# A one-core kernel for a long convolution gated with product-key experts: first loads reordered, first fold ahead of its scale, and another count of matmul time in the recording loop

## The chip, the core and the metric

The kernel runs on one core of a Trainium2 chip, as one program. The metric is the time of one execution on the device in microseconds (us). Five engines work beside each other, each through its own queue of instructions in a fixed order, and meet at semaphores: TensorE (PE; PEld is its loading of weights), VectorE (DVE), ScalarE (ACT), GpSimd (POOL) and SyncE (SP), which here only issues DMA transfers. Matmuls write to PSUM, of which this kernel uses eight banks of 128 x 512 f32.

## What is computed

The input x is one sequence of 2048 tokens with 576 channels. Two results are mixed by a gate.

```python
x = A_u
g = _sigmoid((x * gate_w).sum(-1, keepdims=True))
a = _A_ref(...)   # long convolution along the tokens, by FFT, + u * Dskip
b = _B_ref(...)   # experts
return g * a + (1 - g) * b
```

Part a makes a filter K of 2048 taps for each channel from 128 complex states, `K = einsum("dn,dnl,dn->dl", Cc, exp(logdA * l), dB).real`, and convolves it with the tokens. Part b asks 4096 experts through two tables of 64 keys, for 32 heads:

```python
q = jnp.einsum("nd,dhc->nhc", xf, w_q)
s1 = jnp.einsum("nhd,ed->nhe", q[..., :dk], k1)
s2 = jnp.einsum("nhd,ed->nhe", q[..., dk:], k2)
# the two best of s1 and of s2, the two best of their four sums: expert numbers top_e, weights g
act = _gelu(jnp.einsum("nd,nhkd->nhk", xf, u[top_e]))
out = jnp.einsum("nhk,nhk,nhkd->nd", g, act, v[top_e])
```

## The kernel before

**What is multiplied.** Nearly every product in f32 is made of f16 parts: an operand is scaled by a power of two and split into a high part and a low part (high = scaled value rounded to f16, low = what is left), and three matmuls per 128 of the 576 channels give the product. The last 64 channels go into two more. So a group of scores or of expert products is 14 matmuls of 128 x 512 (`triple`).

**Names.** The reader needs these, since the profile goes by them. `xs`, `xr` are a block of 512 tokens as loaded (first 512 channels, last 64 twice), `xb` the scaled and split block; there are four blocks (tb 0 to 3). `wq` is half a set of 8 columns of query weights (4 x 576 f32), `kt` the keys. Query weights and keys are folded into one matrix before they meet the tokens: matmuls `wb` of `wq` with `kt` (64 x 64 each), then a scale, then the parts `whl` (high, low) and `wrem` (last 64 channels). The scale of a fold needs the sum of squares of the weights (ACT writes `wj` and a sum, TensorE adds it over the partitions in `wn`). `us`, `ur` are 512 expert rows as loaded, `uhl` their parts, `sq` the sum of squares for their scale. `s` is a group of scores (c, t: fold c of 8, token tile t of 16); its reader on VectorE is MAX8 into `m` and FIND_INDEX8 into `i`. `a` is a group of products of tokens and expert rows (c, tb, j); its reader scales it to `go`, which is stored to `g_d` in HBM. `kP`, `CS`, `e`, `Y`, `kb`, `ko` are the steps that generate the filter, 18 pairs of channel chunks, spread over VectorE, ScalarE and GpSimd; `u` and `uh` the first step of the transform of the tokens. Later come `k` (transform of the filter), `pr`, `pi`, `pv` (product of the transforms), `tr` (transposing the chosen indices), `A`, `Be`, `Bg` (one-hot matrices from the indices, built on VectorE), `S` (their product: the weight of each expert), `gl` (gelu of the products, times S), `wh` (its parts), `vhl` (the parts of the expert values), `o` (output, `wh` times `vhl`) and `y` (the last transform of part a, with tables `tf` and rows `yz` loaded from HBM; `ya` is its sum).

**What sets the order.** The kernel is a Python program that records instructions, and the order in which it records them is the order in each engine's queue. A loop over `groups` (128 groups of scores) and `acts` (128 groups of expert products) records TensorE's main stream. It keeps a clock of its own: `mm` adds to `clock[0]` an estimated time for each matmul and a charge where the shape of the stationary operand changes, `Engine` estimates when VectorE, ScalarE and GpSimd are through, `dma` when a transfer lands. All else (building blocks, folds, the filter, the transforms) are generators in a heap; each yields until its operands are ready by these estimates (`ready`) or a bank or slot is free (`need`), and is then resumed by `pump` between matmuls. So the estimates never change what is computed, but they set where each instruction stands. Slots in SBUF (nine of 8 KB per partition) and banks have quotas by tag (`sc`, `kb`, `wb`, `slot`, `raw`).

**The start.** It loads keys, the first half of fold 0's query weights, the constants, token block 0, the second half of the weights and the first expert rows, in that order. `x_build` takes its block as an argument; `x_rest` loads and builds blocks 1 to 3 one after the other once block 0 is done. In `w_half` the matmuls of the fold come after the scale is known and with all banks from one tag.

## Time and profile before

| | |
|---|---|
| median of the runs | 1479.43 us (1478.44 to 1482.02) |
| the profiled execution | 1478.13 us, of which its span 1476.3 us |
| busy, share of the span: TensorE, VectorE, ScalarE, GpSimd | 97%, 85%, 53%, 36% |
| mean granted clock of TensorE | 0.995 |
| idle time of TensorE, sum | 42.0 us |
| HBM read, written | 147.51 MB, 71.30 MB |

Rows of the profile read as follows. A row of the order of time has start, length, engine, line, operation, output <- inputs, shape and count; in square brackets stands how long the engine had been idle and what ended that. Nearly all lines are 213 (matmul), 133 (the other engines) and 204 (DMA), since helpers record everything, so one goes by the tile names. A row of waits has the total in us, how many times, and the longest. A row of a table by stretches has the stretch, its length, the busy time of PE, PEld, DVE, ACT and POOL, each with its number of instructions, then the granted clock of TensorE (1.00 is full), the busy share of the DMA engines and GB/s.

### The profile page before, as it was taken

To read this page: it belongs to the slowest core of one execution; us is meant where nothing else is said; L and a number is where in the kernel's file an instruction comes from. 1 tells how busy PE (TensorE), PEld (TensorE's weight loads), DVE (VectorE), ACT (ScalarE), POOL (GpSimd) and SP (SyncE) were. 2 spreads that over 40 slices of the span, in tenths; PEclk is the share of its full clock that TensorE was granted. 3 is DMA by queue.
4 is the path that set the end of the run, shared out by engine and by line. 5 is a ranking of instruction groups with operands and counts; after the bars stand their busy time and mean duration, and the time that the engine had idled before them with its cause. 6 is when DMAs were issued, how large, how long until landed. Compare 5 with 4: busy or idle time off the path is not lost.

```text
span 1476.3 us, 36780 instructions
## 1 busy us (share of the span) xinstructions
PE 1434.3 (97%) x14024; PEld 861.1 (58%) x14028; DVE 1254.2 (85%) x4589; ACT 786.0 (53%) x1310; POOL 537.7 (36%) x513
## 2 busy tenths in 40 slices
PE   5999999999999999999999999999999999999999
PEld 3444544454455544555554444456787788788787
DVE  6989899989988899598997997589998998898860
ACT  6558778677686866625655644664424324323310
POOL 0454663634726465202247999522010110110100
PEclk9999999999999999999999999999999999999999
DMA  6443542443344343466576758676532442442400
GB/s 227 133 121 103 173 129 76 151 134 94 107 130 147 108 133 122 132 218 234 177 269 228 267 192 258 208 245 186 191 119 92 131 144 70 151 146 67 154 9 17
DMA packets 139184, 221.20 MB, mean 150 GB/s; under 512 B 11648, under 2 KB 82688, under 8 KB 132608
## 3 DMA queue, kind: packets, MB, share of 16 engines
q1 hardware_dynamic: 138912, 218.78, 46.2%
q8 instruction: 110, 1.80, 0.5%
q14 instruction: 66, 0.54, 0.1%
q10 hardware_dynamic: 96, 0.07, 0.0%
HBM read 147.51 MB, written 71.30 MB: 148 GB/s over the span
## 4 chain that ended last, share of the span: by engine, by line
PE 73%; DVE 19%; DMA 3%; ACT 2%; issue 2%; SPq 0%; POOL 0%; DVEq 0%; ACTq 0%
PE o L213 23%; PE a L213 19%; PE s L213 17%; DVE i L133 4%; PE S L213 4%; DVE m L133 3%; PE wb L213 2%; DVE e L133 2%; PE kb L213 2%; DVE uhl L133 2%; PE pr L213 1%; DVE Y L133 1%; DVE CS L133 1%; PE y L213 1%; DVE uh L133 1%
## 5 line engine op out<-in xcount | busy, mean ns | idle before, releaser
L213 PE MATMUL o<-vhl,wh 128*128 128x288 f16 x3072 | 387.3, 286 | 0.0
L213 PE MATMUL s<-whl,xb 128*128 128x512 f16 x1536 | 366.4, 381 | 5.9 <-DVE whl L133 3.5
L213 PE MATMUL a<-xb,uhl 128*128 128x512 f16 x1536 | 362.4, 380 | 4.1 <-DVE i L133 4.1
L213 PEld LDWEIGHTS <-wh 128*128 128x128 f16 x3072 | 295.9, 98 | 76.4 <-issue 3.7
L213 PEld LDWEIGHTS <-xb 128*128 128x128 f16 x1792 | 171.4, 98 | 211.4 <-issue 20.8
L213 PEld LDWEIGHTS <-uhl 128*128 128x128 f16 x1536 | 147.9, 98 | 178.7 <-issue 5.7
L133 DVE FIND_INDEX8 i<-m,s 128x8 uint32<-128x64 f32 x1024 | 206.5, 223 | 0.0
L133 ACT ACTIVATE wh<-gl,s_wg 128x1024 f16<-128x1024 f32 x63 | 67.6, 1137 | 206.8 <-DVE gl L133 206.8
L133 DVE MAX8 m<-s 128x8 f32<-128x64 f32 x1024 | 146.3, 215 | 24.6 <-PE s L213 23.3
L133 POOL TENSOR_TENSOR CS<-CS,ex 128x512 f32<-128x512 f32 x72 | 100.6, 1427 | 153.5 <-DVE ex L133 144.3
L133 POOL TENSOR_TENSOR ya<-ya,db 128x576 f32<-128x576 f32 x16 | 31.8, 1994 | 341.2 <-DVE Bg L133 151.2
L133 DVE SCALAR_TENSOR_TENSOR wh<-gl,s_wg,wh 128x1024 f16<-128x1024 f32 x64 | 90.6, 1447 | 11.3 <-ACT wh L133 11.3
L133 DVE TENSOR_TENSOR gl<-S,gl 128x256 f32<-128x256 f32 x256 | 90.0, 415 | 10.2 <-PE S L213 9.2
L133 POOL TENSOR_TENSOR e<-aN,rt 128x512 f32<-128x512 f32 x72 | 86.4, 1221 | 31.8 <-PE kb L213 31.7
L133 ACT ACTIVATE go<-a,i_a 128x512 f32<-128x512 f32 x95 | 64.4, 683 | 52.1 <-PE a L213 35.2
L133 DVE TENSOR_TENSOR Bg<-Be,vals 128x1024 f16<-128x1024 f16 x128 | 89.6, 741 | 2.2
L133 ACT ACTIVATE gl<-gl 128x1024 f32<-128x1024 f32 x64 | 63.5, 1045 | 44.8 <-DMA gl<-g_d 41.4
L133 DVE TENSOR_TENSOR A<-iota_a,vals 128x2048 f16<-128x2048 f16 x64 | 79.9, 1249 | 0.0
L213 PE MATMUL s<-wrem,xb 128*128 128x512 f16 x256 | 76.7, 381 | 0.1
L213 PE MATMUL a<-xb,wrem 128*128 128x512 f16 x256 | 76.2, 379 | 0.0
L213 PE MATMUL S<-Bg,A 128*128 128x64 f16 x2048 | 73.1, 193 | 2.6 <-DVE Bg L133 2.4
L213 PEld LDWEIGHTS <-A 128*128 128x128 f16 x2048 | 70.8, 97 | 7.7 <-issue 1.8
(202 smaller groups left out, 2225.2 us busy)
## 6 DMA issues: line engine op xcount, KB each, us to landing
g_d<-go SPq DMA_DIRECT2D x128, 256.0 KB, 2.5
gl<-g_d SPq DMA_DIRECT2D x32, 1024.0 KB, 5.7
wq<-in_wq_dram SPq DMA_DIRECT2D x16, 1152.0 KB, 7.1
us<-in_au_dram SPq DMA_DIRECT2D x64, 144.0 KB, 3.0
su_d<-us SPq DMA_DIRECT2D x32, 288.0 KB, 2.7
sk_d<-k1o SPq DMA_DIRECT2D x32, 288.0 KB, 3.0
vn<-in_vv_dram SPq DMA_DIRECT2D x32, 288.0 KB, 3.2
ui<-su_d SPq DMA_DIRECT2D x16, 576.0 KB, 4.2
```

The costliest lines, as they stand in the source:

```text
L133: return f(*a, **k)
L213: T.matmul(o, l, r, start=start, stop=stop)
```

## The change

The diff has four parts.

- The count in `mm`: a change of shape is now told by whether more than 64 rows are used and by 32, 64 or 128 columns, where before every other number of rows or columns was another shape. The charge for coming back to 128 columns is 0.13 instead of 0.15, the estimate of a fold's matmul 0.058 instead of 0.06.
- The order of the first loads: keys, token block 0, both halves of the query weights, expert rows, and the constants last, inside `k_split` once the expert rows are asked for. The f16 copy of the identity follows the constants.
- The fold of c = 0: `w_fold` holds its matmuls, and they are recorded ahead of the scale (three `kb` banks, then one `kb` and two `sc`). For the other folds the order within is as before.
- The blocks of tokens: `x_build` loads its own block, two blocks may be under way (the remainder tile `xr` has two buffers), the squares of block 0 are shared by ScalarE and VectorE, and its scaling goes to VectorE. `x_rest` goes away; `open_u` does its ending.

A last line lets an expert group be recorded late in the run when the next fold isn't ready.

```diff
     def mm(o, l, r, start, stop, cost=None):
-        m = l.shape[0], size(l)
+        m = l.shape[0] > 64, 128 if size(l) > 64 else size(l)
         if m != tiling[0]:
             tiling[0] = m
-            clock[0] += 0.15 if m == (128, 128) else 0.1
+            clock[0] += 0.13 if m == (True, 128) else 0.1
...
-        r = pl.tile([128, 512], F32, tag="xr", name=f"xr{tb}")
+        r = pl.tile([128, 512], F32, tag="xr", name=f"xr{tb}", bufs=2)
...
-    def x_build(tb, a, r):
+    def x_build(tb):
+        while tb and tb - 1 not in scaled:
+            yield 0.3
+        if tb:
+            yield from need("slot", 2)
+            xl[tb] = x_load(tb)
+        a, r = xl.pop(tb)
+        while tb and 0 not in uhl:
+            yield 0.3
         b = slot([9, 512], F16, f"xb{tb}")
         sq = b[:, 0:5].bitcast(BF16)
         yield from ready(a, r)
-        S.activation(sq[:, 0:4, :], a, AF.Square)
+        if tb:
+            S.activation(sq[:, 0:4, :], a, AF.Square)
+        else:
+            S.activation(sq[:, 0:2, :], a[:, 0:2], AF.Square)
+            V.tensor_mul(sq[:, 2:4, :], a[:, 2:4], a[:, 2:4])
...
+        for o, i in [(b[:, k], a[:, k, :]) for k in range(4)] + [(b[:, 8], r)]:
+            if tb == 0 or S.free > V.free + 2.0:
+                V.tensor_scalar(o, i, s, None, op0=OP.mult)
+            else:
+                S.activation(o, i, AF.Copy, scale=s)
+        scaled.append(tb)
...
     def w_half(c, h, w):
         fl = lambda x: x.rearrange("p a b -> p (a b)")
         yield from ready(w)
+        pbs = []
...
+        squared.append(h)
+        if c == 0:
+            yield from w_fold(c, h, w, pbs, ("kb", "kb", "kb") if h == 0 else ("kb", "sc", "sc"))
         yield from ready(junk)
         while not sk:
             yield 0.3
-        tag = side()
+        tag = side() if c else "sc"
...
     dma(kt, kT)
+    xl = {0: x_load(0)}
     w_load(0, 0)
-    dma(cst, cst_d[:, :KT])
-    xl = [x_load(0)]
     w_load(0, 1)
...
         sk.append(1)
+        while 0 not in uraw:
+            yield 0.3
+        dma(cst, cst_d[:, :KT])
+        yield from ready(cst)
         V.tensor_copy(identb, ident)
...
-    spawn(x_build(0, *xl[0]))
-    spawn(u_build(0), 9)
-    spawn(x_rest(), 10)
+    for tb in range(4):
+        spawn(x_build(tb), 3 * tb)
+    spawn(u_build(0), 4)
...
-        a_ok = a_ok and (len(acts) > 26 or not groups)
+        a_ok = a_ok and (len(acts) > 26 or not groups or groups[0][0] not in whl)
```

Since the estimates set the order, the change moves instructions all over the program; the number of instructions on TensorE is the same, and on the other engines a few move from one to another. Three places are shown.

VectorE at the start, ahead of the first row maxima (MAX): the parts of the fold `whl0` from its banks `wb0_h_k` (h the half, k the channels), the parts of token block `xb0` and those of the first expert rows `uhl0`. Before:

```order
L133 TENSOR_SCALAR sci_76<-sci_76 128x1 x2
L133 SCALAR_TENSOR_TENSOR whl0_136<-wb0_1_2_239,sci_76,whl0_136 128x2x256
L133 SCALAR_TENSOR_TENSOR xb0_137<-xs0_122,sci_76,xb0_137 128x512
L133 SCALAR_TENSOR_TENSOR wrem2_116<-wb0_1_4_240,sci_76,wrem2_116 64x128 x2
L133 SCALAR_TENSOR_TENSOR whl0_136<-wb0_1_0_238,sci_76,whl0_136 128x2x256
L133 SCALAR_TENSOR_TENSOR uhl0_230<-us0_150,sci_76,uhl0_230 128x512
L133 SCALAR_TENSOR_TENSOR xb0_137<-xs0_122,sci_76,xb0_137 128x512
L133 SCALAR_TENSOR_TENSOR uhl0_230<-us0_150,sci_76,uhl0_230 128x512
L133 SCALAR_TENSOR_TENSOR xb0_137<-xr0_123,sci_76,xb0_137 64x512
L133 SCALAR_TENSOR_TENSOR uhl0_230<-us0_150,sci_76,uhl0_230 128x512 x2
L133 SCALAR_TENSOR_TENSOR wrem0_114<-ur0_151,sci_76,wrem0_114 64x512
```

After:

```order
L133 TENSOR_REDUCE nu_86<-sq_297 128x1
L133 TENSOR_SCALAR sc_75<-nu_86 128x1
L133 TENSOR_SCALAR sci_76<-sc_75 128x1
L133 TENSOR_SCALAR sci_76<-sci_76 128x1 x2
L133 SCALAR_TENSOR_TENSOR whl0_135<-wb0_1_2_227,sci_76,whl0_135 128x2x256
L133 SCALAR_TENSOR_TENSOR wrem2_116<-wb0_1_4_228,sci_76,wrem2_116 64x128 x2
L133 SCALAR_TENSOR_TENSOR whl0_135<-wb0_0_2_167,sci_76,whl0_135 128x2x256
L133 SCALAR_TENSOR_TENSOR uhl0_282<-us0_142,sci_76,uhl0_282 128x512
L133 SCALAR_TENSOR_TENSOR whl0_135<-wb0_1_0_226,sci_76,whl0_135 128x2x256
L133 SCALAR_TENSOR_TENSOR uhl0_282<-us0_142,sci_76,uhl0_282 128x512 x3
L133 SCALAR_TENSOR_TENSOR wrem0_114<-ur0_143,sci_76,wrem0_114 64x512
```

The token parts have moved ahead of this place, and the last low part of `whl0`, from `wb0_1_0`, now stands behind the first row of `uhl0` instead of ahead of it.

SyncE around the load of the last token block, `xs3`, among the stores of expert products `go0_tb_j`. Before:

```order
L204 DMA g_d_65<-go0_0_3_592 128x4x128
L204 DMA g_d_65<-go0_1_0_662 128x4x128
L204 DMA g_d_65<-go0_1_1_692 128x4x128
L204 DMA g_d_65<-go0_1_2_814 128x4x128
L204 DMA g_d_65<-go0_1_3_832 128x4x128
L204 DMA xs3_841<-in_xT_dram 128x4x512
L204 DMA xr3_842<-in_xT_dram 64x512 x2
L204 DMA wq1_0_905<-in_wq_dram 128x2304
```

After:

```order
L204 DMA g_d_65<-go0_0_3_609 128x4x128
L204 DMA g_d_65<-go0_1_0_681 128x4x128
L204 DMA g_d_65<-go0_1_1_698 128x4x128
L204 DMA xs3_731<-in_xT_dram 128x4x512
L204 DMA xr3_732<-in_xT_dram 64x512 x2
L204 DMA g_d_65<-go0_1_2_720 128x4x128
L204 DMA g_d_65<-go0_1_3_861 128x4x128
L204 DMA wq1_0_923<-in_wq_dram 128x2304
```

The load has moved from behind the store of `go0_1_3` to behind that of `go0_1_1`. On TensorE the norm of that block (`x3`) stands 37 matmuls behind the end of group a0_1_3 before, and 68 behind the end of a0_1_1 after.

VectorE at the entry to the output stage, between the last weights of tile 0 (`gl0`, `wh0`) and the first of tile 15 (`gl15`). Before:

```order
L133 SCALAR_TENSOR_TENSOR vhl6_12548<-vhl7_12549,sci_76,vhl6_12548 128x576 x2
L133 SCALAR_TENSOR_TENSOR wh0_1_13086<-gl0_0_12722,s_wg_92,wh0_0_13085 128x1024
L133 TENSOR_SCALAR go7_1_1_13118<-a7_1_1_13090,i_a_91 128x512
L133 SCALAR_TENSOR_TENSOR vhl7_12549<-vs_12972,sci_76,vhl7_12549 128x576
L133 SCALAR_TENSOR_TENSOR wh0_1_13086<-gl0_0_12722,s_wg_92,wh0_0_13085 128x1024
L133 TENSOR_SCALAR go7_1_2_13143<-a7_1_2_13112,i_a_91 128x512
L133 SCALAR_TENSOR_TENSOR wh0_1_13086<-gl0_1_12723,s_wg_92,wh0_0_13085 128x1024
L133 SCALAR_TENSOR_TENSOR vhl7_12549<-vs_12972,sci_76,vhl7_12549 128x576
L133 TENSOR_TENSOR A115_0_13165<-iota_a_12479,vals_80 128x2048
L133 TENSOR_TENSOR Be15_0_13167<-iota_b_12480,vals_80 128x1024
L133 TENSOR_TENSOR Bg15_0_13169<-Be15_0_13167,vals_80 128x1024 x2
```

After:

```order
L133 TENSOR_TENSOR A115_0_13100<-iota_a_12470,vals_80 128x2048
L133 TENSOR_TENSOR Be15_0_13102<-iota_b_12471,vals_80 128x1024
L133 TENSOR_TENSOR Bg15_0_13104<-Be15_0_13102,vals_80 128x1024 x2
L133 TENSOR_TENSOR A115_1_13107<-iota_a_12470,vals_80 128x2048
L133 TENSOR_TENSOR Be15_1_13109<-iota_b_12471,vals_80 128x1024
L133 TENSOR_TENSOR Bg15_1_13111<-Be15_1_13109,vals_80 128x1024 x2
L133 SCALAR_TENSOR_TENSOR wh0_1_13094<-gl0_0_12547,s_wg_92,wh0_0_13093 128x1024
L133 SCALAR_TENSOR_TENSOR vhl4_12478<-vhl5_12686,sci_76,vhl4_12478 128x576
L133 SCALAR_TENSOR_TENSOR wh0_1_13094<-gl0_0_12547,s_wg_92,wh0_0_13093 128x1024
L133 SCALAR_TENSOR_TENSOR wh0_1_13094<-gl0_1_12548,s_wg_92,wh0_0_13093 128x1024
L133 SCALAR_TENSOR_TENSOR vhl5_12686<-vhl6_12687,sci_76,vhl5_12686 128x576
L133 TENSOR_SCALAR go7_2_0_13218<-a7_2_0_13149,i_a_91 128x512
```

The two one-hot builds of tile 15 have moved ahead of `wh0`, and conversions of the expert values (`vhl`) that were through by then now stand among them. On TensorE all eight blocks S of tiles 0 and 15 now stand ahead of the first output matmul, where it was six, with 15 groups of expert products between the first transposition and there instead of 23.

More of the change, by code (lines that the diff above doesn't have):

```diff
@@ L468, in x_build @@
         xb.append(b)
-    whl, wl, sk, halves = {}, {}, [], {}
+        if tb == 3:
+            V.tensor_reduce(out=nx2, in_=nx, axis=AX, op=OP.max)
+            yield from ready(nx2)
+            open_u()
+    whl, wl, sk, halves, scaled, squared = {}, {}, [], {}, [], []
     side = lambda: "kb" if caps["wb"] == 0 else "wb"
@@ L502, in w_half @@
         o = slice(256 * h, 256 * h + 256)
[L503 to L517 removed]
+        if c:
+            yield from w_fold(c, h, w, pbs, (side(),) * 3)
         for k, tag, pb in pbs:
@@ L1180, in u_load @@
         return a, r
-    uhl, i_u = {}, {}
+    uhl, i_u, uraw = {}, {}, []
     def u_build(c):
@@ L1503, in k_split, with open_u @@
         sk.append(1)
+        while 0 not in uraw:
+            yield 0.3
+        dma(cst, cst_d[:, :KT])
+        yield from ready(cst)
         V.tensor_copy(identb, ident)
-    def x_rest():
+    def open_u():
         nonlocal uf
-        while not xb:
-            yield 0.5
-        for tb in range(1, 4):
-            yield from need("slot", 2)
-            yield from x_build(tb, *x_load(tb))
-        V.tensor_reduce(out=nx2, in_=nx, axis=AX, op=OP.max)
-        yield from ready(nx2)
         PL.__exit__(None, None, None)
```

41 lines of the change are left out of this document (22 added, 19 removed).

## The prediction

> **What bounds the kernel now.** I read the page first, then the waits of TensorE over the whole run, then the order of time at the three places where those waits lie.
>
> ```profile
> span 1476.3 us, 36780 instructions
> ...
> PE 1434.3 (97%) x14024; PEld 861.1 (58%) x14028; DVE 1254.2 (85%) x4589; ACT 786.0 (53%) x1310; POOL 537.7 (36%) x513
> ...
> PE 73%; DVE 19%; DMA 3%; ACT 2%; issue 2%; SPq 0%; POOL 0%; DVEq 0%; ACTq 0%
> ```
>
> TensorE is busy for all but 42.0 of 1476.3 us, and it carries 73% of the chain that ended last. The change neither adds nor removes a matmul (20,810 instructions on TensorE in both orders, form by form), so it can only move those 42 us, the clock, and the wait for the last rows. The next view says who holds TensorE up.
>
> ```profile
> PE wn L213 <- ACT wj L133: 8.8, 4, 4.9
> PE a L213 <- DVE i L133: 4.1, 2, 2.5
> PE s L213 <- DVE whl L133: 3.5, 1, 3.5
> ...
> PE kb L213 <- DVE i L133: 2.7, 1, 2.7
> PE u L213 <- DVE uh L133: 2.5, 2, 1.8
> ...
> PE x L213 <- ACT xb L133: 1.9, 1, 1.9
> ...
> PE y L213 <- DMA tf<-in_tf_dram: 1.2, 1, 1.2
> ```
>
> Columns: total us, times, longest. Two rows (wn, s) belong to the start, before the scores run; a, kb and u lie between 200 and 590 us, where the filter is generated beside scores and expert products; x is the last block of tokens at 88 us; y lies at the entry to the output stage at 1034 us. Each is a term below.
>
> **A. The start.** What matters is when the stream of score matmuls begins, and it needs the folded weights whl of both halves, high and low parts.
>
> ```profile
> 4.15 0.59 SPq L204 DMA_DIRECT2D wq<-in_wq_dram  x1
> ...
> DMA to landing us min/median/max: 5.5/8.0/10.5
> ...
> cst<-in_cst_dram SPq DMA_DIRECT2D x1, 288.0 KB, 5.8
> ...
> wq<-in_wq_dram SPq DMA_DIRECT2D x16, 1152.0 KB, 7.1
> ...
> 14.86 1.16 ACT L133 ACTIVATE wj<-wq 128x1152 bf16<-128x1152 f32 x1
> ...
> 17.31 0.72 ACT L133 ACTIVATE xb<-xs,sci 128x512 f16<-128x512 f32 x1
> 17.97 1.91 ACT L133 ACTIVATE uhl<-us 128x2048 bf16<-128x2048 f32 x1
> ...
> 20.49 0.70 ACT L133 ACTIVATE xb<-xs,sci 128x512 f16<-128x512 f32 x1
> 21.22 1.27 ACT L133 ACTIVATE whl<-wb,sci 128x512 f16<-128x512 f32 x2
> 22.37 1.48 ACT L133 ACTIVATE wrem<-wb,sci 64x128 f16<-64x128 f32 x4
> 23.88 0.72 ACT L133 ACTIVATE uhl<-us,sci 128x512 f16<-128x512 f32 x1
> ...
> 24.30 0.71 DVE L133 SCALAR_TENSOR_TENSOR wrem<-wb,sci,wrem 64x128 f16<-64x128 f32 x2
> 25.02 0.75 DVE L133 SCALAR_TENSOR_TENSOR whl<-wb,sci,whl 128x512 f16<-128x512 f32 x1
> 25.69 0.74 DVE L133 SCALAR_TENSOR_TENSOR uhl<-us,sci,uhl 128x512 f16<-128x512 f32 x1
> ...
> 25.83 4.54 PE L213 MATMUL s<-whl,xb 128*128 128x512 f16 x11 [3.49 <-DVE whl L133]
> ```
>
> Before, the second half of the query weights lands at 4.15 + 10.5 = 14.65 us, and the last low part of whl (25.02) lets TensorE go at 25.83. The diff sends the tokens ahead of both halves and puts the 288 KB of constants behind them, so the second half has 288 KB less ahead of it. That is worth between nothing and 1.4 us (a quarter of the 5.5 us that the first 1152 KB took); I take 0.8, so 13.85. From there ScalarE's queue, in its new order, has: the two squares 2.45 (14.86 to 17.31), one high part 0.58 (half of 21.22 to 22.37), the remainder 1.51 (22.37 to 23.88), the expert squares 2.52 (17.97 to 20.49), two high parts 1.15, and the remainder of the second half 1.51: together 9.72, to 23.6. Then VectorE: remainder pair 0.72, one low part 0.67, the expert row that now stands ahead (its operand, the first scaled expert row, is there at 23.6 + 0.72 = 24.3) 0.67, and the last low part 0.75: 26.4. Against 25.8 that is **+0.6**. What the early tokens gain is not on this path: the token scaling that went from ScalarE to VectorE is done long before. Ends: -0.2 (landing 1.4 earlier, ScalarE still the last) and +1.4 (landing as before). The first fold ahead of its scale, its three banks, the split squares and the later identity cast cost nothing for the same reason; were that cover gone, each would show at its own length, under 1 us.
>
> **B. The last block of tokens.**
>
> ```profile
> 79.99 0.50 SPq L204 DMA_DIRECT2D xs<-in_xT_dram  x1
> ...
> 86.72 1.91 ACT L133 ACTIVATE xb<-xs 128x2048 bf16<-128x2048 f32 x1 [6.56 <-DMA xs<-in_xT_dram]
> ...
> 88.68 1.24 PE L213 MATMUL x<-xb,onesb 128*128 128x512 bf16 x4 [1.90 <-ACT xb L133]
> ```
>
> From issue to norm matmul take 8.7 us. Before, the load stands on SP behind the store of expert group (0,1,3), and TensorE has 37 matmuls (2.6 groups, about 8 us) from that group to the norm. After, the load stands behind (0,1,1), two stores earlier, with 68 matmuls between, at 0.22 us each (a 512-column matmul, as in the first row of C) 15 us. The wait goes: **-1.9**; ends -1.9 and 0. The remainder rows' second buffer lets SP run on past this point, so the filter parameters and the second expert rows queued behind are sooner too, and nobody waits for those.
>
> **C. The count of matmul time.** The count decides how much work the recording loop puts on TensorE beside the filter.
>
> ```profile
> 218.80 0.38 PE L213 MATMUL kP<-rt,wb 96*128 96x512 bf16 x1
> 219.02 1.46 PE L213 MATMUL s<-whl,xb 128*128 128x512 f16 x6
> ```
>
> A kP matmul (96 rows) holds TensorE for 0.22 us, as long as any 512-column one, and nothing more. The old count charged 0.10 on entering that shape and 0.15 on leaving. By its own rule the old order has 265 changes of shape, 32.7 us; by the new rule 162, 18.6 us. So the plan ran 14 us slow on TensorE, which then reached its operands ahead of VectorE. With the slack gone from the plan, the waits a, kb and u (4.1 + 2.7 + 2.5 = 9.3) should shrink. But the whole number of score and expert groups between the first and the last filter product is 123.4 in both orders, with 3 score groups fewer and 4 expert groups more, so the relief is only in how they lie. I take a third: **-3.0**. Ends: -9.3, and +4 should waits be drawn as badly elsewhere.
>
> **D. The entry to the output stage.**
>
> ```profile
> PE S L213 <- DVE Bg L133: 1.6, 2, 1.3
> ...
> 1017.20 0.59 PE L213 MATMUL a<-xb,wrem 128*128 128x512 f16 x2
> ...
> 1024.82 8.25 PE L213 MATMUL o<-vhl,wh 128*128 128x288 f16 x66
> 1034.28 2.15 PE L213 MATMUL y<-yz,tf 128*32 128x288 f32 x32 [1.22 <-DMA tf<-in_tf_dram]
> ```
>
> The first row is the waits from 940 to 1060 us. The loads for y begin once the last expert group is stored; from its end (1017.8) to y are 16.5 us. After, TensorE has only one S block (about 1.0 us) and 96 output matmuls (0.125 each, 12.0) in that time: it waits 3.5 where it waited 1.2, +2.3. Behind y, 54 output matmuls instead of 30 stand ahead of the third one-hot block, 3.0 us more, which covers the 1.6. Net **+0.7**; ends -1.6 and +3.5.
>
> That 3.5 us may also cool the clock. Rows at the one long wait of the middle:
>
> ```profile
> 214.00:215.00 1.00, 0.81 (x33) 0.84 (x37) 1.00 (x3) 0.00 (x0) 1.00 (x2) 0.62 0.00 0
> 215.00:216.00 1.00, 1.00 (x47) 1.00 (x38) 1.00 (x2) 0.00 (x0) 1.00 (x1) 0.50 0.51 170
> 216.00:217.00 1.00, 0.63 (x23) 0.39 (x18) 0.97 (x2) 0.00 (x0) 1.00 (x2) 0.50 0.91 199
> 217.00:218.00 1.00, 1.00 (x58) 1.00 (x48) 1.00 (x2) 0.00 (x0) 1.00 (x1) 0.67 0.78 242
> ```
>
> The sixth number after the stretch's length is the granted clock. After a wait of 2.71 us it fell to half and cost 0.38 + 0.50 + 0.50 + 0.33 = 1.7 us. The Trainium skill, "TensorE: Matmul & The Clock Gate", section "What's actually happening", has the clock halve after an idle window of about 3.4 us that runs freely. By the page a wait of 3.5 may or may not fill a window; by the row it would, and the sum would be 1.7 higher. I leave the 1.7 out of the sum and in the range.
>
> **Sum.** +0.6 - 1.9 - 3.0 + 0.7 = -3.6 us. The profiled execution took 1478.13, 1.30 below the median of 1479.43, so -3.6 gives 1475.8 on the median. A measurement of this kernel tells about 0.3% (4.4 us) from no change, so this is "same" (1475.0 to 1483.9), near its lower edge.
>
> **Rivals.** R1, the start gains what its order suggests: the whole of whl is there when its first piece is (ScalarE at 20.9 + 0.6 = 21.5), and the stream begins 4.3 us earlier instead of 0.6 later: 1475.8 - 4.9 = 1470.9. For it: tokens land some 4 us sooner. Against: ScalarE's queue as summed in A.
>
> R2, the count was the whole cause: all 9.3 us and the 1.7 us of half clock go, 8.0 more than I took: 1467.8. For it: every one of these waits is TensorE ahead of VectorE. Against: the equal 123.4 groups.
>
> R3, slower: VectorE is late at the entry to the output stage. After, 15 expert groups instead of 23 stand between the first transposition and the first output matmul, and all eight one-hot builds of the first two tiles lie there, where it was six.
>
> ```profile
> 965.97 2.38 DVE L133 TENSOR_TENSOR Bg<-Be,vals 128x1024 f16<-128x1024 f16 x2
> ...
> 984.91 1.29 DVE L133 TENSOR_TENSOR Bg<-Be,vals 128x1024 f16<-128x1024 f16 x2
> ```
>
> A Bg pair costs 1.29 us alone and 2.38 when disturbed. Undisturbed, VectorE ends the last build 1.5 us after TensorE wants it, inside the y wait. If each of five builds is stretched by 1.1 us two times over, in Bg and in one of its other two parts, the wait is 12.5; it takes the place of the 3.5 of y (+9.0) and halves the clock (+1.7): 1475.8 + 10.7 = 1486.5. It decides from a wait of about 10 us. The Trainium skill, "Advanced Engine Details and Errata", section "Mode Summary", says that GpSimd and two-port Vector instructions block each other; GpSimd has two more subtractions here than before, so by that rule the stretch is likelier.
>
> **Chances.** The forecast 0.46 (own range 1473 to 1481, so 0.08 of it lies below 1475.0), R1 0.07, R2 0.23, R3 0.24. Faster 0.38, same 0.38, slower 0.24. The range 1466 to 1487 takes in R2 and R3's price and leaves out some 0.15 of their far ends.
>
> **What would show it.** A: the first long row of s starts between 25.6 and 27.2 us, released by VectorE's whl. B: no wait before the last x, at about 80 us. C: the a, kb and u waits between 110 and 590 us sum to 5 to 8 us. D: y waits about 3.5 us for tf, and the wait of S for Bg is under 1 us. I am wrong on A if s starts before 24 us, on C if that sum is under 2 or over 10, and the sign is wrong if TensorE shows more idle time than 42 us.

## The result: 13.4 us faster, and where the time went

The changed kernel takes 1467.09 us (median of 6 runs, 1465.23 to 1469.32), the kernel before 1480.46 us in the same sitting (6 runs, 1478.44 to 1483.74). The ratio is 0.9908, with a 95% interval from 0.9893 to 0.9923: faster by 0.92%, clear of the 0.3% that a measurement of this kernel can tell. I had forecast 1475.8, just inside "same", and had given "faster" and "same" 0.38 each. The time lies inside the range (1466 to 1487), but by 1.1 us only, and it is the time of rival R2 (1467.8) and not of the forecast. That the range held is partly luck, as the stages below show.

The head of the changed kernel's page:

```profile
span 1464.7 us, 36789 instructions
...
PE 1431.2 (98%) x14025; PEld 858.4 (59%) x14028; DVE 1248.5 (85%) x4589; ACT 790.6 (54%) x1315; POOL 532.0 (36%) x511
...
PE 84%; DVE 10%; DMA 3%; ACT 1%; issue 1%; SPq 1%; POOL 1%; DVEq 0%; ACTq 0%; POOLq 0%
```

TensorE's idle time is 33.5 us instead of 42.0, and its busy time is 3.1 us less for the same matmuls. Some 1.2 us of that is the clock: by the granted clock in the two traces, 8.2 us of its busy time lay at half clock instead of 10.6. Where the other 1.9 us come from was not traced. The waits of TensorE in the changed kernel (total, times, longest, in us):

```profile
PE x L213 <- ACT xb L133: 4.5, 1, 4.5
PE S L213 <- DVE Bg L133: 4.2, 6, 2.3
PE s L213 <- DVE whl L133: 4.2, 1, 4.2
PE sq L213 <- ACT uhl L133: 4.0, 1, 4.0
...
PE pi L213 <- DVE m L133: 1.7, 1, 1.7
PE k L213 <- ACT k1o L133: 1.4, 1, 1.4
PE y L213 <- DMA tf<-in_tf_dram: 1.0, 1, 1.0
...
PE u L213 <- DVE uh L133: 0.7, 2, 0.5
```

The waits a and kb for VectorE's i, 6.8 us before, are gone, and u has fallen from 2.5 to 0.7. The x wait here is the first block's norm at 8 us, not the last block's. To see the stages, two tables by stretches, of before and then of after (stretch, length, then busy time of PE, PEld, DVE, ACT, POOL, the granted clock and DMA):

```profile
110.00:630.00 520.00, 508.60 (x5067) 260.35 (x5067) 463.95 (x1761) 381.21 (x564) 271.10 (x217) 1.00 0.41 125
630.00:985.00 355.00, 351.38 (x2991) 176.43 (x2991) 298.03 (x1780) 190.68 (x489) 191.90 (x249) 1.00 0.70 231
985.00:1165.00 180.00, 176.20 (x1999) 132.68 (x1997) 168.81 (x267) 65.03 (x72) 20.59 (x11) 1.00 0.47 150
```

```profile
110.00:630.00 520.00, 517.18 (x5052) 262.73 (x5051) 463.83 (x1713) 385.50 (x570) 270.83 (x218) 1.00 0.43 130
630.00:985.00 355.00, 351.37 (x3117) 178.51 (x3116) 294.86 (x1818) 190.94 (x488) 183.97 (x243) 1.00 0.67 224
985.00:1165.00 180.00, 173.84 (x1985) 133.24 (x1984) 171.95 (x261) 77.13 (x86) 24.46 (x15) 1.00 0.48 154
```

While the filter is generated (110 to 630 us) TensorE idles 2.8 us instead of 11.4. At the entry to the output stage it idles 6.2 instead of 3.8. But the same stretch of time holds different work in the two orders, so I also use a measure that does not depend on it. Each matmul counts with the usual interval from its start to the next one's (0.216 us for 512 columns, 0.1225 for 288, 0.0303 for an S, 0.0138 for a kb, and so on, taken from rows without waits). The loss up to a point is the time passed less the work done. Losses taken between equal amounts of work compare two orders stage by stage, and hold waits and slow clock together. The stages are named by their times in the kernel before:

```
us lost by TensorE          to 32  32-110  110-630  630-985  985-1165   all
before                      21.8     2.8     19.7      5.7      5.1     55.3
after                       22.3     0.0      9.3      4.2      7.9     43.8
difference                  +0.5    -2.8    -10.4     -1.5     +2.8    -11.5
```

The last column also holds the 0.1 to 0.3 us lost behind 1165 us. Its difference of -11.5 us is that of the two profiled executions (1478.13 and 1466.58); the other 1.9 of the 13.4 us lie between these executions and the medians and belong to no stage here. So nearly all of the gain is in the filter stage, 2.8 us are in the token blocks, and the start gives nothing.

### The profile page after: what moved, and what is told of

Its sections match the earlier page's. It is cut to its first block, busy times and chain, and to the rows that moved or that the text cites. A ratio compares the mean times of both kernels' runs of the same rounds, so it can differ in the third digit from the quotient of the medians.

```text
span 1464.7 us, 36789 instructions
## 1 busy us (share of the span) xinstructions
PE 1431.2 (98%) x14025; PEld 858.4 (59%) x14028; DVE 1248.5 (85%) x4589; ACT 790.6 (54%) x1315; POOL 532.0 (36%) x511
## 4 chain that ended last, share of the span: by engine, by line
PE 84%; DVE 10%; DMA 3%; ACT 1%; issue 1%; SPq 1%; POOL 1%; DVEq 0%; ACTq 0%; POOLq 0%
PE o L213 24%; PE a L213 23%; PE s L213 22%; PE S L213 4%; PE wb L213 2%; PE kb L213 2%; DVE i L133 2%; PE pr L213 2%; DVE m L133 1%; PE u L213 1%; PE y L213 1%; PE kP L213 1%; DVE e L133 1%; PE pv L213 1%; DVE uh L133 1%
## 5 line engine op out<-in xcount | busy, mean ns | idle before, releaser
L133 ACT ACTIVATE gl<-gl 128x1024 f32<-128x1024 f32 x64 | 63.5, 1045 | 34.8 <-DMA gl<-g_d 34.8
L213 PEld LDWEIGHTS <-A 128*128 128x128 f16 x2048 | 70.6, 97 | 11.2 <-DVE Bg L133 4.1
```

What stands on the lines that cost most here:

```text
L133: return f(*a, **k)
L213: T.matmul(o, l, r, start=start, stop=stop)
```

## The experiments

I started with two theories. "Pace": the old count makes the plan late, so TensorE meets operands that VectorE has not made, and mending the count removes the waits. "Draw": the waits are chance meetings in one particular order, so that any other order draws others. For "pace" spoke the clock that the recording loop keeps, read at the end of each score or expert group, beside the time of the same group in the trace. Before, the plan is 1.8 us late at the first group, 14.7 at the 64th, 19.9 at the 160th. In the changed kernel, read at every eighth group, it is never more than 1.9 us off up to the 224th.

The losses of all orders that were run, by the same stages, with the median time and the ratio to the kernel before:

```
us lost by TensorE          to 32  32-110  110-630  630-985  985-1165   all   median    ratio (95%)
before                      21.8     2.8     19.7      5.7      5.1     55.3  1480.46
after                       22.3     0.0      9.3      4.2      7.9     43.8  1467.09  0.9908 (0.9893-0.9923)
e1_count_alone              20.0     3.3     17.5      9.0      9.7     59.8  1483.67  1.0023 (1.0013-1.0033)
e2_count_undone             24.2     1.2     14.4      6.7     12.3     58.9  1481.61  1.0013 (1.0003-1.0023)
e3_old_rule_cheaper         22.5     3.0     12.5     13.0     15.0     66.2  1491.04  1.0085 (1.0068-1.0102)
e4_late_rule_undone         22.4     0.0      9.6     16.3      5.0     53.5  1474.65  0.9963 (0.9949-0.9977)
d11_charge                  22.7     0.0     11.2      4.2     17.6     56.0  1478.37  0.9979 (0.9968-0.9990)
d15_charge                  22.6     0.0     10.9     13.3      6.4     53.4  1470.44  0.9925 (0.9910-0.9940)
d20_charge                  22.3     0.0     15.8      6.5      3.5     48.3  1470.85  0.9928 (0.9908-0.9948)
e7_expert_rows_later        20.2    11.9     13.9      9.0      4.5     59.8  1485.07  1.0031 (1.0014-1.0047)
f3_load_order_undone        25.4     0.0      6.4      4.0     20.7     56.8  1477.78  0.9981 (0.9967-0.9995)
f1_onehot_cost              22.9     0.0      9.3      2.4     19.6     54.4  1477.18  0.9976 (0.9965-0.9987)
f2_charge_20_late           22.7     0.0      9.3      8.7      5.1     45.9  1468.08  0.9916 (0.9892-0.9939)
g1_charge_20_at_entry       22.3     0.0      9.1      4.1     10.6     46.4  1470.08  0.9935 (0.9921-0.9948)
```

A stage's loss is that of one execution. How far it repeats can be read from the five orders that are equal up to about 600 us (after, e4, f1, f2, g1): 9.1 to 9.6 us in the filter stage. The profiled execution of d15 was longer than most of its runs (1476.50 us against a median of 1470.44), so its total stands some 6 us above its usual run.

### The count by itself, and the count undone

e1: the kernel before with the new count alone.

```diff
-        m = l.shape[0], size(l)
+        m = l.shape[0] > 64, 128 if size(l) > 64 else size(l)
...
-            clock[0] += 0.15 if m == (128, 128) else 0.1
+            clock[0] += 0.13 if m == (True, 128) else 0.1
...
-                        mm(pb[64 * hh:64 * hh + 64, cs], w[:, gh, d:d + 64], rhs, True, True, 0.06)
+                        mm(pb[64 * hh:64 * hh + 64, cs], w[:, gh, d:d + 64], rhs, True, True, 0.058)
```

> The kernel before with the new count alone (rule, charge, and a fold's matmul at 0.058). Theory 'pace': the old count runs ahead of the chip (compared group by group, its clock stands 15 us too late at the 64th group and 20 us at the 160th), so TensorE is sent work whose operands VectorE has not made, and this draws the a, kb and u waits. Then those waits between 110 and 590 us fall from 11.3 us to under 4, and the time is 1470 to 1473 us: the wait of x (1.9) stays. Theory 'draw': the waits are chance meetings in one order, and the fast result comes from the sum of the parts or from luck; then the time is 1475 to 1483 us.

Measured: 1483.67 us, the ratio 1.0023 (1.0013 to 1.0033), so no gain and if anything a little slower. The waits for i are still there, at other places, and the entry to the output stage has become worse:

```profile
PE a L213 <- DVE i L133: 7.5, 5, 2.0
PE S L213 <- DVE Bg L133: 7.4, 8, 1.9
```

In the filter stage the count alone saves 2.2 us (19.7 to 17.5), no more than what I had forecast for it (3.0), and the later stages take back 7.9. "Pace" as I stated it is refuted: it wanted filter waits under 4 us.

e2: the changed kernel with the old count (the diff of e1 the other way round).

> The changed kernel with the old count in it (old rule, 0.15, and a fold's matmul at 0.06); loads, start and blocks of tokens stay changed. 'Pace': the plan runs late again, the filter's waits between 110 and 590 us are 7 us or more, and the time is 1475 to 1479 us. 'Draw': any order can be as good, 1466 to 1473 us.

Measured: 1481.61 us, the ratio 1.0013 (1.0003 to 1.0023). All of the gain is gone. In the filter stage 5.1 of the 10.4 us are lost again (9.3 to 14.4), which agrees with "pace" in kind; the rest comes back at the entry (12.3 instead of 7.9), at the start (24.2 instead of 22.3) and in the stages between. So in these two orders neither the count nor the rest of the change brings the gain without the other. In the filter stage they bring 2.2 and 5.3 us alone, and 10.4 together; each figure is that of one order, and orders scatter by several us, as the next runs show.

e3: the old rule, with charges that add up to what the new count charges.

```diff
-            clock[0] += 0.15 if m == (128, 128) else 0.1
+            clock[0] += 0.085 if m == (128, 128) else 0.057
```

> The kernel before with the old rule of shapes, but both charges at 0.57 of what they were (0.085 and 0.057), so that the sum over the run is what the new count charges (18.6 us). 'Pace': the sum decides and not which changes are charged; filter waits under 5 us, time 1469 to 1474 us. If it has to be the right changes that are charged (kP's 96 rows cost nothing): 1475 to 1482 us. 'Draw': anything from 1467 to 1485 us.

Measured: 1491.04 us, the ratio 1.0085 (1.0068 to 1.0102), slower than every theory had it, "draw" with its 1467 to 1485 included. The filter stage did gain (19.7 to 12.5), with the old start and the old rule. The two later stages lost 17.2 us more than before. That is the first sign that these two stages decide about as much as the filter does, and by something that none of my terms held.

### The line that I had not priced

e4: the changed kernel without the added condition on late expert groups.

```diff
-        a_ok = a_ok and (len(acts) > 26 or not groups or groups[0][0] not in whl)
+        a_ok = a_ok and (len(acts) > 26 or not groups)
```

> The changed kernel without the added condition on late expert groups. If that line is what brought the waits at the entry to the output stage (S and y, 6.0 us, against 3.7 before): they fall to 3 to 4 and the time is 1464 to 1466 us. If the line does nothing there: 1466 to 1469 us. If it is what keeps TensorE fed while the last folds are made (690 to 930 us): 1469 to 1474 us.

Measured: 1474.65 us, the ratio 0.9963 (0.9949 to 0.9977), 7.6 us above the changed kernel. The two orders are the same up to some 620 us. Then the next fold is not ready, expert groups are held back at 26 left, and TensorE has nothing to do. Its order of time in this kernel:

```profile
626.74 0.16 PE L213 MATMUL wn<-sc,onesb 128*128 128x1 bf16 x1 [1.92 <-ACT wj L133]
628.03 0.16 PE L213 MATMUL wn<-sc,onesb 128*128 128x1 bf16 x1 [1.12 <-ACT wj L133]
634.03 2.53 PE L213 MATMUL s<-whl,xb 128*128 128x512 f16 x11 [1.74 <-DVE whl L133]
706.57 1.11 PE L213 MATMUL k<-ksb,tk 128*128 128x288 f16 x4 [3.52 <-DVE k1o L133]
```

With the line, four expert groups fill this hole (22 are left afterwards instead of 26), and the stage from 630 to 985 us loses 4.2 instead of 16.3. Of these 12.1 us some 6.5 lie in the hole itself (between 618 and 640 us TensorE idles 4.8 us and has half clock for 3.4); the rest are later waits of that order, such as the one of k. The price is paid at the entry to the output stage, which has four groups fewer to cover VectorE: 7.9 instead of 5.0. In the kernel before and in e1 the line would change nothing at all: with it, the two orders are instruction by instruction the same, since there no fold is missing once 26 groups or fewer are left. It is worth some 8 us only in the order that the rest of the change makes. My prediction carried no term for it.

### How sharp is the count

Three kernels have one other number each, the charge for coming back to 128 columns; as an example d11:

```diff
-            clock[0] += 0.13 if m == (True, 128) else 0.1
+            clock[0] += 0.11 if m == (True, 128) else 0.1
```

> The changed kernel with one number changed, the charge for coming back to 128 columns, 0.11 instead of 0.13: 80 such charges or so, 1.6 us over the whole run, far less than any clock of the plan is right to. Theory 'fit': the losses follow how well the count fits the chip, so this order is as good as the changed one, 1465 to 1470 us, with 8 to 11 us lost by TensorE between 110 and 630 us (before: 19.7, changed: 9.3). Theory 'draw': each new order draws its own waits; the time lies anywhere between 1464 and 1483 us and the stage losses scatter by 4 us or more.

> The changed kernel with a charge of 0.15, 1.6 us over the run to the other side. 'Fit': 1465 to 1471 us, 8 to 12 us lost between 110 and 630 us. 'Draw': anywhere between 1464 and 1483 us, and not in one line with 0.11, 0.13 and 0.20.

> The changed kernel with a charge of 0.20, some 5.6 us too much over the run, a third of the old count's error. 'Fit': worse than 0.13 and 0.15, 12 to 15 us lost between 110 and 630 us and 1470 to 1476 us. 'Draw': no order in the four; it may as well be the best of them.

Measured: 1478.37, 1470.44 and 1470.85 us with 0.11, 0.15 and 0.20, against 1467.09 with 0.13. In the filter stage the losses stand as "fit" would have them: 11.2, 9.3, 10.9 and 15.8 us at 0.11, 0.13, 0.15 and 0.20, and 14.4 with the old count in e2. That is one order per charge, and two more orders at 0.13 lose 13.9 and 6.4 us there (e7 and f3 below), so a fit is likely at most and not shown. In the last two stages together there is no order at all: 21.8, 12.1, 19.7 and 10.0 us. A change of 0.02 us in a charge, which is nothing as an estimate, moved the time by 11 us (d11).

### The start

e7: expert rows held back until the folded weights are complete. The changed kernel already holds their squares back until both halves of the weights are squared (`len(squared) < 2`), a line of the change that the list of its parts does not name.

```diff
-        while len(squared) < 2:
+        while len(squared) < 2 or c == 0 and 0 not in whl:
             yield 0.3
```

> The changed kernel with the squares and parts of the first expert rows held back until the folded weights whl of c = 0 are complete. By the sum of part A of the prediction these two items stand ahead of the last part of whl: 2.52 us of squares on ScalarE and 0.67 us of an expert row on VectorE, so the stream of s starts 3.2 us earlier, at 23.2 us instead of 26.3. If the start is bound by something else (landing of the weights, the scale), it stays at 25 to 26.5 us. The time: 3 us less if the order behind it holds its luck, 1463 to 1465; by 'draw' the orders behind it are new as well, and the time may lie anywhere between 1462 and 1480 us though the start gains.

Measured: 1485.07 us, the ratio 1.0031 (1.0014 to 1.0047). The stream of s does start earlier, at 23.98 us instead of 26.34, so the items that part A summed are what stood in its way (2.4 us of the 3.2). But the expert rows and the token blocks then come late, one after the other:

```profile
23.98 4.78 PE L213 MATMUL s<-whl,xb 128*128 128x512 f16 x11 [4.58 <-DVE whl L133]
...
44.67 0.39 PE L213 MATMUL a<-xb,wrem 128*128 128x512 f16 x1 [1.20 <-DVE wrem L133]
...
61.05 0.61 PE L213 MATMUL s<-wrem,xb 128*128 128x512 f16 x2 [1.42 <-DVE xb L133]
...
88.67 0.61 PE L213 MATMUL s<-wrem,xb 128*128 128x512 f16 x2 [1.42 <-DVE xb L133]
```

The stage from 32 to 110 us loses 11.9 us instead of nothing, which is more than the start can give.

f3: the changed kernel with the old order of the first loads.

```diff
     dma(kt, kT)
-    xl = {0: x_load(0)}
     w_load(0, 0)
+    dma(cst, cst_d[:, :KT])
+    xl = {0: x_load(0)}
     w_load(0, 1)
...
-        while 0 not in uraw:
-            yield 0.3
-        dma(cst, cst_d[:, :KT])
-        yield from ready(cst)
         V.tensor_copy(identb, ident)
...
-    spawn(u_build(0), 4)
+    spawn(u_build(0), 9)
```

> The changed kernel with the old order of the first loads (first half of the weights, constants, tokens, second half, expert rows) and the expert rows asked for as late as before; the new way of building the token blocks, the fold ahead of its scale and the new count stay. If the gain of 2.8 us between 32 and 110 us is due to the way the blocks are built, it stays (0 to 0.5 us lost there); if to the early tokens, 2 to 3 us are lost again. The start loses 20 to 23 us either way. 'Fit': the filter stage loses 9 to 12 us; if instead the low filter loss hangs on this one order of the start, it goes back towards the 17.5 of the count alone.

Measured: 1477.78 us, the ratio 0.9981 (0.9967 to 0.9995). The stream of s starts at 28.72 us, so with the fold ahead of its scale the new order of loads, with the expert rows asked for sooner, is worth 3.1 us (25.4 against 22.3); together they leave the start where it was. From 32 to 110 us nothing is lost, so the 2.8 us of the token blocks come from the new way of building them and not from the early tokens. The filter stage loses 6.4 us, the least of all orders. Its total is high for the entry to the output stage above all.

### The entry to the output stage

f1: only the estimate of VectorE's f16 products changes, and with it only the order from the first transposition on (947 us).

```diff
-        return 0.07 + n * (0.00053 if out.dtype == F16 and not psum and op != "scalar_tensor_tensor" else 0.00104) + wait
+        return 0.07 + n * (0.00065 if out.dtype == F16 and not psum and op != "scalar_tensor_tensor" else 0.00104) + wait
```

> The changed kernel with one estimate of VectorE's raised, that of the f16 one-hot products (A, Be, Bg): 0.65 ns per element instead of 0.53, which makes Bg 0.74 us and A 1.40 (the trace has 0.91 and 1.34 at the entry to the output stage). The order is the changed kernel's up to the first transposition (about 947 us), so only the entry is drawn anew. If the S waits there (4.9 us in all, VectorE busy without a gap from 985 to 1060 us) come from the plan counting VectorE too fast, TensorE is given other work there and loses 4 to 5 us between 985 and 1165 us instead of 7.9: 1463 to 1465 us. If VectorE is simply the bound of that stretch, nothing is won by another order: 6 to 10 us, 1465 to 1470. 'Draw': 3 to 18 us there, as the orders measured so far have, 1462 to 1478.

Measured: 1477.18 us, the ratio 0.9976 (0.9965 to 0.9987). With the same order up to 947 us, the entry loses 19.6 us instead of 7.9, beyond the 3 to 18 that "draw" allowed. Of the 11.7 us more, 5.4 are idle time of TensorE (11.5 instead of 6.2), and half clock makes up about the rest. This is where the run shows what an entry is made of. TensorE's order of time in f1:

```profile
1008.46 0.23 PE L213 MATMUL S<-Bg,A 128*128 128x64 f16 x1 [3.77 <-DVE Bg L133]
1009.05 1.81 PE L213 MATMUL S<-Bg,A 128*128 128x64 f16 x31 [0.36 <-DVE Bg L133]
...
1046.11 0.24 PE L213 MATMUL S<-Bg,A 128*128 128x64 f16 x1 [3.91 <-DVE Bg L133]
```

VectorE ahead of the second of these waits, and GpSimd beside it, in the same kernel:

```profile
1035.73 0.69 DVE L133 TENSOR_TENSOR Be<-iota_b,vals 128x1024 f16<-128x1024 f16 x1
1036.45 3.46 DVE L133 TENSOR_TENSOR Bg<-Be,vals 128x1024 f16<-128x1024 f16 x2
1039.83 2.44 DVE L133 SCALAR_TENSOR_TENSOR wh<-gl,s_wg,wh 128x1024 f16<-128x1024 f32 x1
...
1045.36 1.29 DVE L133 TENSOR_TENSOR Bg<-Be,vals 128x1024 f16<-128x1024 f16 x2
```

```profile
1036.01 1.54 POOL L133 TENSOR_TENSOR vhl<-vs,vhl 128x576 f16<-128x576 f32 x1 [12.50 <-ACT vs L133]
1037.51 3.67 POOL L133 TENSOR_TENSOR ya<-ya,db 128x576 f32<-128x576 f32 x2
```

From 1036.0 to 1041.2 us GpSimd works, and in that time VectorE's pair of Bg takes 3.46 us (1.29 at 1045) and the part of wh 2.44 (1.28 at 1029 in the same kernel): 3.3 us lost on VectorE, which has no gap there, and TensorE waits 3.91 for Bg. Over the 14 traces this leaves little room for another cause: 1601 single Bg without GpSimd beside them took 0.69 us at most, and of 191 beside it some took up to 2.62. The orders f3 and d11 have it too: GpSimd's ya and vhl beside A, Be and Bg, and S waits of 6.02 and 3.96 us behind. The stretch is 2.0 us ahead of the first wait of f1, 2.6 in f3 and 3.3 in d11, so it makes a part of these waits; the rest is VectorE's own work standing ahead. In f3 and d11 TensorE then waits another 5.3 and 3.2 us for vhl from GpSimd itself. In the changed kernel GpSimd has two short subtractions there, and the longest wait is 2.26:

```profile
1003.81 1.10 PE L213 MATMUL S<-Bg,A 128*128 128x64 f16 x31 [0.40 <-DVE Bg L133]
1007.61 0.20 PE L213 MATMUL S<-Bg,A 128*128 128x64 f16 x1 [2.26 <-DVE Bg L133]
1008.21 1.10 PE L213 MATMUL S<-Bg,A 128*128 128x64 f16 x31 [0.39 <-DVE Bg L133]
1022.09 2.15 PE L213 MATMUL y<-yz,tf 128*32 128x288 f32 x32 [1.03 <-DMA tf<-in_tf_dram]
1031.13 1.13 PE L213 MATMUL S<-Bg,A 128*128 128x64 f16 x32 [0.67 <-DVE ya L133]
```

The Trainium skill, "Advanced Engine Details and Errata", section "Mode Summary", says that GpSimd and Vector instructions that use two ports block each other. The stretch in f1 (Bg from 1.29 to 3.46 us a pair) looks like such a block; whether Bg uses two ports, no run here shows.

A longer wait also costs a second time. The table by stretches of f1 and then of the changed kernel, around the first of these waits:

```profile
1007.00:1009.00 2.00, 0.23 (x1) 0.13 (x2) 1.97 (x4) 0.00 (x0) 0.13 (x1) 0.69 0.61 194
1009.00:1012.00 3.00, 2.95 (x37) 2.48 (x37) 2.96 (x8) 0.78 (x1) 0.00 (x0) 0.50 0.12 39
1012.00:1016.00 4.00, 4.00 (x24) 2.69 (x23) 4.00 (x11) 1.57 (x2) 0.00 (x0) 0.68 0.67 196
```

```profile
1009.00:1012.00 3.00, 3.00 (x34) 2.43 (x31) 3.00 (x7) 0.78 (x1) 0.00 (x0) 1.00 0.26 80
1012.00:1016.00 4.00, 4.00 (x35) 3.19 (x34) 3.93 (x11) 2.42 (x3) 0.46 (x1) 1.00 0.68 180
```

After 3.77 us of waiting the clock is at half, and that costs 0.50 x 3 + 0.32 x 4 = 2.8 us more; after 2.26 us it stays full. Waits of 3.91 (f1), 3.95 (g1) and 6.02 (f3) us were followed by half clock too. But the length of a wait alone does not decide it. In all 14 traces the granted clock changes only on a grid of 3.41 us: any two changes in a trace lie a whole number of 3.41 us apart. Between the start and the last rows it fell 29 times, each time at the end of a window of that grid in which TensorE had been busy for 0.55 of the time or less (26 of them 0.47 or less); of the windows at full clock without a fall the least busy had 0.44. The wait of 2.26 us lies across a border of the grid. The two windows that share it, and then the window of the 3.77 us in f1:

```profile
1003.14:1006.55 3.41, 1.74 (x34) 1.15 (x34) 3.41 (x8) 1.24 (x3) 1.56 (x1) 1.00 0.99 308
1006.55:1009.97 3.42, 1.97 (x39) 1.73 (x40) 3.38 (x5) 0.18 (x1) 0.00 (x0) 1.00 0.39 119
```

```profile
1004.34:1007.75 3.41, 0.35 (x12) 0.22 (x8) 3.38 (x5) 1.39 (x3) 1.93 (x1) 1.00 0.97 323
```

TensorE is busy for 0.51 and 0.58 of the first two, and for 0.10 of the third. The Trainium skill, "TensorE: Matmul & The Clock Gate", section "What's actually happening", has the clock halve after an idle window of some 3.4 us that runs freely. Length and grid agree; but a window here need not be idle throughout.

f2: the charge of 0.20 once the filter is made. g1: the same charge only from the transpositions on.

```diff
-            clock[0] += 0.13 if m == (True, 128) else 0.1
+            clock[0] += (0.2 if kdone[0] == NCK else 0.13) if m == (True, 128) else 0.1
```

```diff
-            clock[0] += 0.13 if m == (True, 128) else 0.1
+            clock[0] += (0.2 if gated else 0.13) if m == (True, 128) else 0.1
```

> The changed kernel with the charge of 0.20 used only once the filter is made; up to there the order is that of the changed kernel. The filter stage keeps its loss of 9.3 to 9.6 us between 110 and 630 us in either theory. If 0.20 fits the two later stages better by itself (9.9 us lost from 630 to 1165 us in the kernel with 0.20 throughout, 12.0 in the changed kernel), the time is 1463 to 1466 us. By 'draw' these two stages lose anything from 10 to 28 us, as they have over ten orders, 1465 to 1483 us.

> The changed kernel with the charge of 0.20 only from the point where all indices are chosen (about 946 us); the order up to there is the changed kernel's, so only the entry to the output stage is drawn anew. Over four orders the loss between 985 and 1165 us has fallen with the charge in force there: 17.6 at 0.11, 7.9 at 0.13, 6.4 at 0.15, 3.5 and 5.1 at 0.20. If that is a fit (the plan runs TensorE too fast against VectorE there), the loss is 3 to 6 us and the time 1463 to 1465 us, below both kernels. If the four are draws, the loss lies anywhere between 3 and 21 us, as over the twelve orders measured, and the time between 1462 and 1480 us.

Measured: 1468.08 us for f2, the ratio 0.9916 (0.9892 to 0.9939), which cannot be told from the changed kernel; and 1470.08 us for g1, 0.9935 (0.9921 to 0.9948). Before g1 the loss at the entry seemed to fall with the charge (17.6, 7.9, 6.4, 3.5 and 5.1). In g1 it is 10.6 where a fit asked for 3 to 6, so that row of five does not hold, and "draw" is what is left. None of the twelve orders beats the changed kernel.

## Why the prediction was right, and where it was not

**A, the start: right, and its sum too.** I had the first long row of s at 26.4 us; it starts at 26.34, released by whl:

```profile
20.84 0.16 PE L213 MATMUL sq<-sc,onesb 128*128 128x2 bf16 x1 [4.04 <-ACT uhl L133]
21.55 0.59 PE L213 MATMUL s<-whl,xb 128*128 128x512 f16 x1 [0.55 <-ACT whl L133]
26.34 4.50 PE L213 MATMUL s<-whl,xb 128*128 128x512 f16 x11 [4.20 <-DVE whl L133]
```

That is +0.5 us at this row, and +0.5 in the loss up to 32 us (forecast +0.6). The terms hold as well as their sum: ScalarE gets the second half of the weights at 13.65 (13.85 in the sum) and is through its items at 23.45 (23.6), and VectorE's last part of whl stands behind the expert row and ends at 26.29:

```profile
13.65 1.16 ACT L133 ACTIVATE wj<-wq 128x1152 bf16<-128x1152 f32 x1 [0.31 <-DMA wq<-in_wq_dram]
25.54 0.75 DVE L133 SCALAR_TENSOR_TENSOR whl<-wb,sci,whl 128x512 f16<-128x512 f32 x1
```
R1, which had the start gain 4.3 us, is refuted. e7 shows that the items summed were the ones in the way, f3 that the order of loads is worth 3.1 us, which the rest of the new start eats.

**B, the last block of tokens: right.** No wait stands before its norm, and the stage from 32 to 110 us loses nothing instead of 2.8 (forecast -1.9 for the wait alone, which was also the end of its range; TensorE's idle time there fell by 2.1 us, and the rest was not traced). f3 shows that the way of building the blocks does it.

**C, the filter: the sign right, the size wrong, -10.4 instead of -3.0.** This is the step that failed, the third that I took of the waits. I had the end of the range at -9.3, the whole of the waits, and R2 added the 1.7 us of half clock; that is what happened in size. The waits of a, kb and u between 110 and 590 us, which I had at 5 to 8 us, sum to 2.1, of which 1.1 are for VectorE. I had set R2 at 0.23 and taken a third, with the argument that between the first and the last filter product both orders have 123.4 groups, "so the relief is only in how they lie". How they lie is all of it: with as many groups between the first and the last kb (3.6 score groups fewer and 3.6 expert groups more), TensorE idles 2.4 us there instead of 11.4. I had also read this term as the work of the count alone, as R2 had. e1 shows that the count alone saves 2.2 us there, e2 that the rest of the change saves 5.3 without it. Why the new token blocks help the filter stage, 100 us and more behind them, was not settled. What the runs show is that four different orders with them and with a charge from 0.11 to 0.15 (the changed kernel's, d11, d15, f3) lose 6.4 to 11.2 us there, and the orders that lack one of the two, or have the charge of 0.20, lose 12.5 to 19.7. e7 has both and loses 13.9; that its late expert rows are the reason was not tried.

**D, the entry: the sign right, the size and the way wrong, +2.8 instead of +0.7.** I let y wait 3.5 us for tf and the S waits vanish. y waits 1.03, less than before (1.22), and S waits 4.9 in all instead of 2.4. The way from the last expert product (it ends at 1005.34) to y is as forecast, 16.7 us against 16.5, and TensorE waits 3.7 of them; but 2.65 of that stand ahead of S, and S waits 2.3 us more outside of it, where I had none. VectorE did not end its builds in time. That is the lateness of R3, but without the stretch that R3 built its price on:

```profile
1006.86 1.29 DVE L133 TENSOR_TENSOR Bg<-Be,vals 128x1024 f16<-128x1024 f16 x2
```

This is the pair for which S waits 2.26 us, and it takes 1.29 as alone. R3's whole price, 10.7 us, fell due in the neighbours f1 (11.7 us more than the changed kernel at the entry), d11 (9.7) and f3 (12.8). I had R3 decide from a wait of about 10 us in all, and that fits them: TensorE idles 11.5, 9.9 and 13.4 us there, and half clock adds the rest.

**What I left out.** The added line on late expert groups had no term. By e4 it is worth 7.6 us net, since without it the changed order would have lost 16.3 us between 630 and 985 us, where the kernel before lost 5.7. Without the line the time is 1474.65, close to my 1475.8, but for other reasons: C's greater gain would have been spent there.

**What the total is made of.** -2.8 for the blocks is a gain of the change that every order with them and the new count shows, e7 with its late rows excepted. Most of -10.4 in the filter stage probably is as well, by the four orders named under C, but e7 does not fit and the cause there stays open. The last two stages are a draw as far as these runs go: over the fourteen orders (e4's by its edit) they lose 10.0 to 28.0 us together, and both kernels of the comparison (10.8 and 12.1) are second and third lowest of them. Had the changed kernel drawn the middle of the others, some 19 us, it would have come out about 7 us slower than it did, near e4, and the range would have held with room.

## What to carry to other kernels

When estimates set the order of instructions, a change of them has two effects: a part that neighbouring orders share (here the 2.8 us of the token blocks and, probably, most of the filter's gain) and a draw, which here was worth up to 11 us for 0.02 us in one charge. Price both, and tell them apart by running neighbours and comparing them stage by stage at equal work, not by the total time. A rule that only bites when a buffer of ready work runs low looks inert in the old order and may be worth most in the new one: follow how much fill-in work is left at each stage before pricing it at nothing.

## What the runs showed of the hardware

The stretch beside GpSimd is not limited to the f16 products: in f1 the f32 part of wh (scalar_tensor_tensor, 1024 elements) took 2.44 us beside GpSimd and 1.28 without. Over the 14 traces 687 such parts without GpSimd beside them took 1.29 us at most.

Half clock can follow a wait well under 3 us. In the kernel before, a wait of 1.60 us in the product of the transforms (64 x 64 f32) was followed by it:

```profile
848.30 0.43 PE L213 MATMUL pi<-ui,cst 64*64 64x256 f32 x2 [1.60 <-DVE m L133]
```

```profile
848.00:850.00 2.00, 1.70 (x20) 1.06 (x20) 2.00 (x19) 0.87 (x2) 1.84 (x5) 0.78 0.73 285
850.00:852.00 2.00, 2.00 (x7) 0.61 (x6) 2.00 (x8) 0.79 (x3) 1.92 (x3) 0.50 0.97 297
```

Its window of the grid of 3.41 us (845.71 to 849.12) has TensorE busy for 0.53. The changed kernel has the same at 888.9 us (a wait of 1.67, a window with 0.51). f1, with the same order there, has the same wait of 1.67 at 889.4, but it falls into windows with 0.83 and 0.68, and the clock stays full. Small matmuls are not needed: in d20 a wait of 1.96 us before products of 512 columns was followed by half clock, at the end of a window with TensorE busy for 1.45 of 3.41 us:

```profile
555.79:559.20 3.41, 1.45 (x8) 0.48 (x7) 3.41 (x27) 0.69 (x1) 3.29 (x3) 1.00 0.36 105
```

So where a wait lies on the grid counts beside its length. Where the border between 0.44 and 0.55 lies, and what counts as busy, is not settled; the three falls above 0.47 all follow f32 products on 64 rows.
